# Expert layers: which engine makes the low parts of the weight blocks, and when the router's ranks are issued

## The chip, the cores and the metric

The kernel runs on one core of a Trainium2 chip. The core's engines work side by side, each through its own queue in order: TensorE (matmuls; PE, and PEld for its weight loads), VectorE (DVE), ScalarE (ACT), GpSimd (POOL) and SyncE (SP, which here issues DMAs). They wait for one another through semaphores. The metric is the device time of one execution in microseconds; the time before is a median of three runs.

## What is computed

```python
def reference(**kwargs):
    attn_out = _attn_ref(r, k, v, w, u)          # a recurrence over 768 steps, 4 x 8 heads of 48
    x = attn_out.transpose(0, 2, 1, 3).reshape(3072, 384)
    x = _moe_ref(x, w_gate, w1, w2)              # first expert layer
    return _moe2_ref(x, modality_id, w_gate, modality_bias, w1, w2)   # second one

def _moe_ref(x, w_gate, w1, w2):
    logits = x @ w_gate                          # second layer: + modality_bias[modality_id]
    expert_idx = np.argmax(logits, axis=1)       # one of 8 experts for each token
    gate_w = softmax(logits) at expert_idx
    for e in range(8):
        mask = expert_idx == e
        h = np.maximum(x[mask] @ w1[e], 0.0)     # 384 -> 1024
        out[mask] = gate_w[mask, None] * (h @ w2[e])   # 1024 -> 384
```

## The kernel before

Attention (class `Attn`) runs first, in an order written out by hand (`manual_schedule`), over 24 steps. The two expert layers (class `Moe`) follow; their first pieces are already issued among the last steps of attention. Outside the part ordered by hand, the compiler's list scheduler may move an instruction within its engine's queue ahead of earlier ones that are not ready in its own simulation; what follows is the program's order.

Tokens are sorted by expert into tiles: big ones of 256 tokens ("b") and small ones of 128 ("s"). Layer one has 12 big and 4 small, layer two 12 big and 1 small; three big tiles of each layer are "early", planned from the tokens known by then. Each tile needs its expert's weights: 8 blocks of 128 x 768 float32. `Moe.load` (L375) fetches a block into one of five `raw` buffers on SP's queue. `Moe.split` (L384) then makes two matrices of it that TensorE can multiply fast: the high part `hi`, a rounded copy by ScalarE (L395), and the low part `lo = raw - hi` (L397), by GpSimd for some blocks and by VectorE for the others:

```python
POOL_LO = (1, 3, 5, 7)                                                      # L32
eng = nc.gpsimd if ch in ((1, 4) if short else POOL_LO) else nc.vector      # L396
eng.tensor_tensor(lo[:, s], raw, hi[:, s].bitcast(F32), op=ALU.subtract)    # L397
```

`short` is set in small tiles. The low part is the last reader of its raw buffer. There are two weight buffers, so in `Moe.run` (L484) the blocks of the next tile are split (`sp`) while the present one is multiplied: in a big tile two after each of the blocks 3 and 4 of the first product and two after each half of the second; in a small one 2, 3 and 3.

A big tile is four blocks of the first product (`g1_big`, L425: 18 matmuls; ScalarE makes the high part of h, L440, VectorE the low one, L441), then two halves of the second product (`g2`, L468: 24 matmuls each; ScalarE writes y, L482). Between them `mid` issues gathers of later tiles (`gather`, L399, indirect DMAs on GpSimd's queue) and turns the next tile's tokens (`xprep`, L406). A small tile is `g1_small`, `ht_small` and one `g2`.

Behind the first three blocks and the two halves stands a `tick` (four ticks in a small tile). Each tick runs one piece of the tile before this one (`prev`, from `post1` or `post2`) and two pieces of the planning (`side`). What is left of `prev` is run at the tile's end. In layer one `post1` (L1022) routes the tile's results for layer two with `Router.group` (L125): a piece ends at each `yield`. The pieces of a two-row tile are: transposes (L135); logits (L141); turning them back, maximum, `rt_eq` and the one-hot `oh` (L148 to L167); the ranks `R` on TensorE from `oh` (L170 to L173) and the running sums; and a last piece with slots, `ol` (L196) and the gate (L200), after which the rows are written to `x2s` on SP's queue (L1026). When all tiles of a set have been routed, `early` or `plan` works out which tokens and which expert each tile of layer two has; the loads and gathers of those tiles come after it. All of the router's small products use one PSUM buffer (`pl`).

`moe.open` is False while attention is issued and True from then on.

Of the kernel before, what the change touches and what calls it, by code (L numbers as in the profile page):

```python
# [13 lines left out]
AF = mybir.ActivationFunctionType  # L14
# [17 lines left out]
POOL_LO = (1, 3, 5, 7)  # L32
# [9 lines left out]
def drain(g):  # L42
    for _ in g:
        pass
# [39 lines left out]
def bc(ap, shape):  # L84
    return ap.to_broadcast(shape)


class Router:
# [36 lines left out]
    def group(self, sp, pt, pl, rows, n, k, act, N=4, bias=None, tok=None):  # L125

        nc, c, v = self.nc, self.c, self.nc.vector
# [36 lines left out]
        if tok is not None:  # L164
            val = sp.tile([P, N, 1], F32, name="rt_val", bufs=2)[:, :n]
            v.tensor_scalar(val, tok, float(NTOK), None, op0=ALU.is_lt)
            v.tensor_tensor(oh, oh, bc(val, sh), op=ALU.mult)  # L167
        yield
        R = pl.tile([P, 512], F32, name="pl")[:, :n * E].rearrange("p (a e) -> p a e", a=n)
        nc.tensor.matmul(R, c.tri, oh, start=True, stop=False)  # L170
# [26 lines left out]
        s = sp.tile([P, N, 1], F32, name="rt_s", bufs=2)[:, :n]  # L197
# [168 lines left out]
class Moe:  # L366
# [14 lines left out]
        raw = t.raw[ch] = self.bufs.get("raw")  # L381
        nc.sync.dma_start(raw, t.w[bass.ds(t.er * P, P), ch * CW:(ch + 1) * CW])

    def split(self, t, ch, short=False):  # L384
        nc = self.nc
        if ch == 0:
            w = self.bufs.get("w")
            t.wt = (w[:, 0, :], w[:, 1, :])
        hi, lo = t.wt
        raw = t.raw.pop(ch)  # L390
        s = slice(ch * CW, (ch + 1) * CW)
        if short and ch in ():
            nc.vector.tensor_copy(hi[:, s], raw)
        else:
            nc.scalar.activation(hi[:, s], raw, AF.Copy)  # L395
        eng = nc.gpsimd if ch in ((1, 4) if short else POOL_LO) else nc.vector  # L396
        eng.tensor_tensor(lo[:, s], raw, hi[:, s].bitcast(F32), op=ALU.subtract)  # L397

    def gather(self, t):  # L399
# [84 lines left out]
    def run(self, tiles):  # L484

        seq = [(t, ch) for t in tiles for ch in range(NCH)]
        pos, nl, ng = [0], [0], [0]

        def ahead():
            while nl[0] < min(len(seq), pos[0] + len(self.bufs.ring["raw"])) and seq[nl[0]][0].known("ei"):  # L490
                self.load(*seq[nl[0]])
                nl[0] += 1

        def sp(k=1, short=False):
            for _ in range(k):
                ahead()
                if pos[0] < len(seq):
                    assert pos[0] < nl[0]
                    self.split(*seq[pos[0]], short)
                    pos[0] += 1  # L500
                ahead()

        def gathers(i):
            while ng[0] < len(tiles) and ng[0] <= i and tiles[ng[0]].known() and (ng[0] < NEARLY or self.open):
                self.gather(tiles[ng[0]])
                ng[0] += 1

        def tick():
            for _ in range(self.PT):
                next(prev, None)  # L510
            for _ in range(self.ST):
                next(self.side, None)

        ahead()
        gathers(1)
        yield
        sp(2 if tiles[0].kind == "b" else NCH)
        yield
        gathers(1)
        yield  # L520
        self.xprep(tiles[0])
        yield
        first = True
        prev = iter(())
        for i, t in enumerate(tiles):
            nxt = tiles[i + 1] if i + 1 < len(tiles) else None
            self.hook(t)
            h = self.new_h()

            def mid():  # L530
                if nxt and not nxt.known():
                    drain(self.side)
                gathers(i + 2)
                if nxt:
                    assert ng[0] > i + 1
                    self.xprep(nxt)
            gathers(i + 1)
            if t.kind == "b":
                for fp in range(4):
                    if first and fp > 0:  # L540
                        sp(2)
                    self.g1_big(t, fp, h)
                    if fp < 3:
                        tick()
                    if not first:
                        sp(0 if fp < 2 else 2)
                    yield
                if first:
                    sp(2)
                while not self.open:  # L550
                    yield
                mid()
                yield
                self.g2(t, 0, h)
                tick()
                sp(2)
                yield
                self.g2(t, 1, h)
                tick()
                sp(4 if first else 2)  # L560
                yield
            else:
                ready = nxt and nxt.known()
                if ready:
                    mid()
                h0 = self.g1_small(t, 0)
                tick()
                h1 = self.g1_small(t, 1)
                self.ht_small(0, h0, h)
                self.ht_small(1, h1, h)  # L570
                tick()
                sp(2, True)
                tick()
                self.g2(t, 0, h, 0, 4)
                if not ready:
                    mid()
                sp(3, True)
                self.g2(t, 0, h, 4, 8)
                tick()
                sp(3, True)  # L580
                yield
            for _ in prev:
                next(self.side, None)
            while i + 2 < len(tiles) and not tiles[i + 2].known("hi"):
                next(self.side)
            prev = t.post(t)
            first = False
        for _ in prev:
            pass
# [410 lines left out]
def build(tc, nc, dm, tk, u, uw, wg1, W1, mod, wg2, bias, W2, out):  # L1000
    NBU, NSU1, NSU2 = 12, 4, 1
    v = nc.vector
    with ExitStack() as ctx:
# [42 lines left out]
        with ExitStack() as ac:  # L1046
# [67 lines left out]
            def tail():  # L1114
                early = r1.early(wk, pl)
                yield next(early)
                moe.bufs.add(pool("mright", 1, mst, side="right"), w=1, raw=3, xg=2, x=2, h=1, y=1)
                run = moe.run(seq1 + seq2)
                yield next(run)
                yield next(early)  # L1120
                yield next(run)
                yield from early
                yield from run
# [143 lines left out]
```

## Time and profile before

| | |
|---|---|
| time, median of 3 | 770.69 us (770.32 to 772.57) |
| the profiled execution's own time | 773.58 us |
| its span, first to last instruction | 771.7 us |
| busy in the span: TensorE | 687.5 us, 89% |
| VectorE | 555.3 us, 72% |
| ScalarE | 421.0 us, 55% |
| GpSimd | 405.7 us, 53% |
| mean granted clock of TensorE | 0.95 |
| low parts on GpSimd / on VectorE | 108 / 124 |

Busy time of an engine includes time in which an instruction has started and stands still. Matmuls are pipelined, and their ends are modelled. The share of the granted clock is that of full speed; its two levels are 1.2 and 2.4 GHz. A wait is put down to what came last ahead of it. Layer one lies at about 240 to 550 us of the span, layer two behind it.

### The profile page before, as it was taken

What the parts mean: (1) busy time and instruction counts of PE and PEld (TensorE: products, weight loads), DVE (VectorE), ACT (ScalarE), POOL (GpSimd) and SP (SyncE); (2) the same over time, 40 slices, a digit from 0 to 9 for tenths busy, and PEclk for the clock granted to TensorE, in tenths of its full rate; (3) what the DMA queues carried; (4) which work ended last, traced back from release to release, by engine and by line L of the source; (5) the groups of instructions that cost most, each with busy time, mean ns of one, the idle gap of its engine ahead of it and who ended that gap; (6) DMA issues with size and microseconds to landing.
All of it is one profiled execution on the core that took longest, in us unless ns stands there. A gap on an engine that the chain in (4) does not pass through costs nothing.

```text
span 771.7 us, 15530 instructions
## 1 busy us (share of the span) xinstructions
PE 687.5 (89%) x5528; PEld 625.1 (81%) x5528; DVE 555.3 (72%) x1149; ACT 421.0 (55%) x805; POOL 405.7 (53%) x318
## 2 busy tenths in 40 slices
PE   3788898799699897999899999889998999999992
PEld 1477676687498787999898898868997999999992
DVE  6799888988666787876887878868863766655410
ACT  2357465653444674667576665546364755566520
POOL 4676544453423674553645454345459876676610
PEclk9689899999799998999999999989998999999996
DMA  8695645512645685865775874574377877676400
GB/s 203 179 289 156 180 115 161 175 51 91 200 126 185 215 282 198 267 201 184 247 245 155 260 250 151 199 232 134 106 256 248 278 223 228 224 226 200 151 31 8
DMA packets 55198, 144.91 MB, mean 188 GB/s; under 512 B 6890, under 2 KB 15740, under 8 KB 55112
## 3 DMA queue, kind: packets, MB, share of 16 engines
q1 hardware_dynamic: 50120, 128.26, 53.8%
q0 software_dynamic: 4992, 15.58, 6.3%
q8 instruction: 45, 0.74, 0.4%
q14 instruction: 41, 0.34, 0.1%
HBM read 125.16 MB, written 18.84 MB: 187 GB/s over the span
## 4 chain that ended last, share of the span: by engine, by line
PE 41%; DVE 12%; DMA 6%; issue 4%; ACT 2%; POOL 2%; SPq 1%; POOLq 0%; ACTq 0%
PE py L477 19%; PE pg L436 17%; DMA raw<-in_W_dram 4%; DVE w L397 4%; DVE rt_eq L158 2%; ACT w L395 2%; DVE rt_L L152 2%; DMA out_dram<-y,si 1%; PE pt L416 1%; PE pg L452 1%; POOL w L397 1%; DVE h L441 1%; PE pl L141 1%; POOL xg L404 1%; DMA xg<-x2s,idxe 1%
## 5 line engine op out<-in xcount | busy, mean ns | idle before, releaser
L397 POOL TENSOR_TENSOR w<-raw,w 128x768 fp32r<-128x768 f32 x108 | 207.5, 1928 | 148.2 <-ACT w L395 140.1
L395 ACT ACTIVATE w<-raw 128x768 fp32r<-128x768 f32 x232 | 194.7, 846 | 134.3 <-DMA raw<-in_W_dram 59.7
L477 PE MATMUL py<-w,h 128*128 128x384 f32 x1272 | 242.4, 343 | 5.8 <-ACT h L440 3.0
L397 DVE TENSOR_TENSOR w<-raw,w 128x768 fp32r<-128x768 f32 x124 | 169.6, 1369 | 104.0 <-ACT w L395 103.4
L436 PE MATMUL pg<-x,w 128*128 128x256 f32 x1728 | 231.8, 289 | 2.9 <-DVE h L441 2.2
L477 PEld LDWEIGHTS py<-w,h 128*128 128x128 f32 x1272 | 221.9, 191 | 9.9 <-ACT h L440 3.2
L436 PEld LDWEIGHTS pg<-x,w 128*128 128x128 f32 x1728 | 218.6, 194 | 8.8 <-issue 3.5
L441 DVE SCALAR_TENSOR_TENSOR h<-pg,h 128x512 fp32r<-128x512 f32 x96 | 64.8, 681 | 11.4 <-ACT h L440 11.1
L440 ACT ACTIVATE h<-pg 128x512 fp32r<-128x512 f32 x96 | 56.1, 586 | 14.2 <-PE pg L436 14.2
L1032 POOL DMA_INDIRECT out_dram<-y,si x25 | 31.6, 1264 | 42.1 <-ACT y L482 32.7
L678 POOL TENSOR_TENSOR K<-dm,G 112x512 f32<-112x512 f32 x24 | 28.4, 1185 | 46.9 <-DVE G L671 15.7
L733 PE MATMUL pg<-R,K 64*128 64x128 f32 (+1 forms) x384 | 38.3, 303 | 16.2 <-DVE vd L723 13.9
L733 PEld LDWEIGHTS pg<-R,K 64*128 64x128 f32 (+1 forms) x384 | 30.9, 201 | 26.6 <-DVE vd L723 16.3
L482 ACT ACTIVATE y<-py,xg 128x384 f32<-128x384 f32 x53 | 30.4, 575 | 34.7 <-PE py L477 26.8
L693 POOL TENSOR_TENSOR R<-dm,Fw 112x512 f32<-112x512 f32 x23 | 29.2, 1268 | 36.7 <-DVE Fw L690 34.2
L404 POOL DMA_INDIRECT xg<-xd,idx x22 | 24.3, 1104 | 26.1 <-DVE rt_eq L158 18.5
L128 ACT ACTIVATE lxT<-pt 128x512 f32<-128x512 f32 (+2 forms) x47 | 22.9, 520 | 23.2 <-PE pt L135 23.2
L690 DVE TENSOR_TENSOR_SCAN Fw<-dm,d1r 112x520 f32<-112x520 f32 x24 | 35.0, 1460 | 0.1
L671 DVE TENSOR_TENSOR_SCAN G<-dm,d1k 112x520 f32<-112x520 f32 x24 | 32.9, 1371 | 2.7 <-DMA dm<-in_dm_dram 2.2
L683 POOL TENSOR_TENSOR rk<-dm 112x512 f32<-112x512 f32 x24 | 33.5, 1397 | 0.0
L750 ACT ACTIVATE KT<-pt 128x448 f32<-128x448 f32 x20 | 10.9, 545 | 41.3 <-PE pt L748 41.3
L739 DVE TENSOR_TENSOR M<-pg,mask 128x512 f32<-128x512 f32 x48 | 30.8, 681 | 0.9 <-PE pg L733 0.4
(204 smaller groups left out, 895.8 us busy)
## 6 DMA issues: line engine op xcount, KB each, us to landing
raw<-in_W_dram SPq DMA_DIRECT2D x232, 384.0 KB, 3.8
dm<-in_dm_dram SPq DMA_DIRECT2D x23, 675.5 KB, 4.9
va<-in_tk_dram SPq DMA_DIRECT2D x24, 256.0 KB, 4.2
x2s<-y SPq DMA_DIRECT2D x12, 400.0 KB, 3.1
xd<-x SPq DMA_DIRECT2D x5, 800.0 KB, 4.5
x2s<-z SPq DMA_DIRECT2D x16, 200.0 KB, 5.8
xd<-x SPq DMA_DIRECT2D x2, 400.0 KB, 2.7
x2s<-y SPq DMA_DIRECT2D x4, 200.0 KB, 3.9
```

Of the source, the lines that this page charges most:

```text
L395: nc.scalar.activation(hi[:, s], raw, AF.Copy)
L397: eng.tensor_tensor(lo[:, s], raw, hi[:, s].bitcast(F32), op=ALU.subtract)
L404: self.nc.gpsimd.indirect_dma_start(t.xg[:, a, :], None, t.src, bass.IndirectOffsetOnAxis(ap=idx, axis=0))
L436: nc.tensor.matmul(ps[:, fi, :], w[:, s], x[:, k].rearrange("p a t -> p (a t)"), start=(n == 0), stop=(n == 8))
L440: nc.scalar.activation(hi, ps, AF.Relu)
L441: nc.vector.scalar_tensor_tensor(lo, ps, 0.0, hi.bitcast(F32), op0=ALU.max, op1=ALU.subtract)
L477: nc.tensor.matmul(ps, x[:, f, a, :], w[:, s], start=(f == 0 and i == 0), stop=(f == 7 and i == 2))
L671: v.tensor_tensor_scan(G[:, ::-1], s.w[:, ::-1], self.d1k[:, ::-1], 0.0, op0=ALU.mult, op1=ALU.add)
L683: self.nc.gpsimd.tensor_tensor(s.rk, s.r, s.k, op=ALU.mult)
L690: v.tensor_tensor_scan(Fw, s.w, s.d1, 0.0, op0=ALU.mult, op1=ALU.add)
L733: nc.tensor.matmul(s.ps[h][:, p * P:(p + 1) * P], s.K[rows, p, :], s.R[rows, p, :], start=True, stop=True)
L1032: nc.gpsimd.indirect_dma_start(out, bass.IndirectOffsetOnAxis(ap=si[:, a_:a_ + 1], axis=0), t.y[:, a_, :D], None, bounds_check=NTOK - 1, o ...
```

## The change

Once `open` is True, the low parts of all blocks are made by VectorE; until then the blocks in `POOL_LO` stay on GpSimd, as before. The argument `short` goes, with a branch that was never taken. In `Router.group`, for the second layer's router alone (`tok is not None`), a second `yield` stands between `oh` and the ranks, so that one piece is empty and the ranks and the last piece are issued one tick later.

```diff
@@ Router.group
             v.tensor_scalar(val, tok, float(NTOK), None, op0=ALU.is_lt)
             v.tensor_tensor(oh, oh, bc(val, sh), op=ALU.mult)
+            yield
         yield
         R = pl.tile([P, 512], F32, name="pl")[:, :n * E].rearrange("p (a e) -> p a e", a=n)
         nc.tensor.matmul(R, c.tri, oh, start=True, stop=False)
@@ Moe.split
-    def split(self, t, ch, short=False):
+    def split(self, t, ch):
...
-        if short and ch in ():
-            nc.vector.tensor_copy(hi[:, s], raw)
-        else:
-            nc.scalar.activation(hi[:, s], raw, AF.Copy)
-        eng = nc.gpsimd if ch in ((1, 4) if short else POOL_LO) else nc.vector
+        nc.scalar.activation(hi[:, s], raw, AF.Copy)
+        eng = nc.gpsimd if ch in POOL_LO and not self.open else nc.vector
         eng.tensor_tensor(lo[:, s], raw, hi[:, s].bitcast(F32), op=ALU.subtract)
@@ Moe.run
-        def sp(k=1, short=False):
+        def sp(k=1):
...
-                    self.split(*seq[pos[0]], short)
+                    self.split(*seq[pos[0]])
...
-                sp(2, True)
+                sp(2)
...
-                sp(3, True)
+                sp(3)
...
-                sp(3, True)
+                sp(3)
```

## Rows read from the trace of the kernel before

**Rows 1.** Busy time by stage: stretch, its length, each engine, clock, DMA, GB/s

```profile
240.00:560.00 320.00, 294.65 (x2065) 273.81 (x2064) 254.06 (x582) 190.51 (x331) 161.60 (x109) 0.98 0.66 210
560.00:600.00 40.00, 36.79 (x266) 35.79 (x265) 21.74 (x37) 23.43 (x38) 29.09 (x21) 0.91 0.79 257
600.00:740.00 140.00, 140.00 (x1005) 140.00 (x1004) 83.19 (x88) 82.66 (x126) 95.81 (x59) 1.00 0.66 208
```

**Rows 2.** TensorE's waits, 240 to 560 us: total us, times, longest

```profile
PE pl L170 <- DVE oh L167: 13.4, 9, 4.5
PE pt L416 <- DMA xg<-x2s,idxe: 3.2, 2, 2.1
PE pg L436 <- DVE h L441: 1.9, 2, 1.0
```

**Rows 3.** TensorE's waits, 560 to 760 us

```profile
PE py L477 <- ACT h L440: 3.0, 1, 3.0
```

**Rows 4.** Timeline, 642 to 650 us: start, us, engine, line, operation [idle before]

```profile
642.07 0.96 DVE L397 TENSOR_TENSOR w<-raw,w 128x768 fp32r<-128x768 f32 x1 [2.81 <-ACT w L395]
...
644.23 0.99 POOL L404 DMA_INDIRECT xg<-x2s,idx  x1 [0.31 <-issue]
...
645.23 1.86 POOL L397 TENSOR_TENSOR w<-raw,w 128x768 fp32r<-128x768 f32 x1
645.30 2.62 DVE L397 TENSOR_TENSOR w<-raw,w 128x768 fp32r<-128x768 f32 x1 [2.27 <-ACT w L395]
...
649.17 2.37 PE L436 MATMUL pg<-x,w 128*128 128x256 f32 x18
```

**Rows 5.** Groups by line: times, busy us, mean ns, idle before and its releasers

```profile
L397 POOL TENSOR_TENSOR w<-raw,w 128x768 fp32r<-128x768 f32 x108 | 207.5, 1928 | 148.2 <-ACT w L395 140.1 <-PE pl L173 4.3 <-DMA raw<-in_W_dram 3.1
...
L397 DVE TENSOR_TENSOR w<-raw,w 128x768 fp32r<-128x768 f32 x124 | 169.6, 1369 | 104.0 <-ACT w L395 103.4
...
L158 DVE SCALAR_TENSOR_TENSOR rt_eq<-rt_L,eneg 128x16 f32<-128x16 f32 x14 | 15.4, 1100 | 0.3
...
L152 DVE TENSOR_TENSOR rt_L<-rt_L,xg 128x16 f32<-128x16 f32 x12 | 9.1, 755 | 0.2
```

**Rows 6.** Timeline, 419 to 425 us: one late `oh`

```profile
419.62 3.94 DVE L158 SCALAR_TENSOR_TENSOR rt_eq<-rt_L,eneg 128x16 f32<-128x16 f32 x1
419.88 3.63 POOL L397 TENSOR_TENSOR w<-raw,w 128x768 fp32r<-128x768 f32 x2
...
424.24 0.18 PE L170 MATMUL pl<-oh,tri 128*128 128x16 bf16 x1 [1.65 <-DVE oh L167]
```

**Rows 7.** Busy time of line 397 alone by stage: VectorE, GpSimd, clock, DMA, GB/s

```profile
240.00:560.00 320.00, 98.89 (x77) 120.11 (x62) 0.98 0.66 210
600.00:740.00 140.00, 52.94 (x32) 61.04 (x32) 1.00 0.66 208
```

**Rows 8.** Timeline, 581 to 595 us: a run of low parts and a stall

```profile
581.42 5.46 POOL L397 TENSOR_TENSOR w<-raw,w 128x768 fp32r<-128x768 f32 x3
...
587.03 0.85 ACT L395 ACTIVATE w<-raw 128x768 fp32r<-128x768 f32 x1 [5.58 <-DMA raw<-in_W_dram]
...
594.28 4.21 PE L436 MATMUL pg<-x,w 128*128 128x256 f32 x18 [0.26 <-DVE h L441]
```

**Rows 9.** Timeline, 418 to 420 us: a gather beside a low part

```profile
418.06 0.94 DVE L397 TENSOR_TENSOR w<-raw,w 128x768 fp32r<-128x768 f32 x1
418.24 1.63 POOL L404 DMA_INDIRECT xg<-xd,idx  x1 [0.81 <-DVE rt_m L155]
```

**Rows 10.** Busy time and clock, 295 to 305 us, columns as rows 1

```profile
295.00:305.00 10.00, 8.62 (x38) 7.96 (x38) 6.96 (x21) 1.99 (x3) 0.88 (x3) 0.66 0.68 233
```

**Rows 11.** Waits of VectorE, GpSimd and ScalarE, 240 to 560 us

```profile
DVE w L397 <- ACT w L395: 39.0, 35, 2.7
POOL w L397 <- ACT w L395: 91.3, 34, 8.3
ACT y L482 <- DMA x2s<-y: 7.7, 4, 2.2
```

## The prediction

> **What bounds the kernel now.** I read the stage table first, because the average over the whole span mixes an attention half, in which the changed lines hardly run, with two expert layers that have different limits. From 600 to 740 us TensorE is busy for 140.00 of 140 us at full granted clock: the second layer, once its plan exists, is bound by TensorE, and nothing that VectorE or GpSimd do faster is worth anything there. From 240 to 560 us TensorE is busy for 294.65 of 320, and from 560 to 600 for 36.79 of 40, at 0.98 and 0.91 of the granted clock [rows 1]. So 25.4 + 3.2 = 28.6 us of idle TensorE, and a few more of slowed clock, are all that this change can win.
>
> Then I asked what ended that idle time. In 240 to 560 us the largest entry by far is the first matmul of the router's ranks (L170) waiting for the one-hot tile `oh` of VectorE (L167): 13.4 us in nine waits. The gathers of the second layer's first tile follow with 3.2 us, the low part of h with 1.9 [rows 2]. After 560 us one wait of 3.0 us for ScalarE's h stands out [rows 3].
>
> Last I asked why VectorE is late, although it is not full. A low part on VectorE alone takes 0.96 us. The one at 645.30, beside a GpSimd low part that began 0.07 us earlier and took 1.86, took 2.62: VectorE stood still until GpSimd was through, and then did its work [rows 4]. The group rows carry the same: 1369 ns in the mean for 124 low parts on VectorE against 0.96 us alone, and `rt_eq`, an operation on 16 elements, has a mean of 1100 ns [rows 5]. One of these explains a wait of TensorE from end to end: `rt_eq` began at 419.62, two GpSimd low parts ran from 419.88 to 423.51, `rt_eq` ended at 423.56, and the rank matmul, which needed `oh` three small operations later, began at 424.24 after 1.65 us of idle [rows 6]. So GpSimd's low parts cost VectorE much of the time that they keep from its queue.
>
> **Part 1: the low parts move to VectorE.** Of 108 on GpSimd those of the blocks split while `open` is still False stay: the first tile's four, and one of the second's if its first two blocks are still issued then. About 103 move; each takes 1928 ns on GpSimd [rows 5] and 0.96 on VectorE [rows 4].
>
> What that does to VectorE's load in the first layer: 98.89 us for 77 low parts, with 62 more on GpSimd [rows 7]. Afterwards 139 x 0.96 = 133.4, so 34.6 more. Against it stand the stalls of other operations: `rt_eq` goes from 1100 to about 170 ns, 14 x 0.93 = 13.0 less; the bias addition `rt_L` from 755 to about 160 ns, 12 x 0.6 = 7.2 less [rows 5]. So 254.06 + 34.6 - 20.2 = 268.5 us at most, and less by whatever the remaining small operations lose to GpSimd now, which I estimate at up to as much again, 20: 248 to 268, as against 254 now. VectorE is no fuller than before; the same time is spent on work rather than on standing still. In the steady second layer it goes from 83.19 to 83.19 - 52.94 + 64 x 0.96 = 91.7 of 140 us [rows 1, 7], under a TensorE that is full: nothing. If that cover failed, and each of the eight tiles there had one low part of h behind one more low part, it would cost 8 x 0.96 = 8 us; the range has room for it.
>
> The raw buffers come free sooner, since the low part is their last reader and takes half as long. That matters where three GpSimd low parts in a row (5.46 us from 581.42) held buffers: ScalarE then stood 5.58 us for the next raw block, its h was queued behind that block, and TensorE idled 3.0 us. After it, 18 matmuls took 4.21 us which elsewhere take 2.37 [rows 3, 4, 8]; the granted clock of this stretch is 0.91 [rows 1]. This stall costs 3.0 + 1.8 = 4.8 us, and goes: the three low parts would take 2.9 us on VectorE, which is busy for 21.74 of the 40 us [rows 1]. Should the raw blocks' own transfers be late next, 0 to 4.8 of it would stay; I take 0, because the wait followed GpSimd's run of three at once.
>
> GpSimd keeps its copies and indirect transfers. A gather overlapped by a VectorE low part took 1.63 us against 0.99 alone [rows 4, 9], so up to 0.64 more for each. It is issued a tile ahead; this shows only at the hand-over between layers, where two gathers in a row are waited for: 0 to 1.3 us.
>
> The Trainium skill speaks to that last price. SBUF — State Buffer, section "Who interferes with whom", says that a two-input VectorE operation takes only the read side of the pair that it shares with GpSimd, so that writing descriptors should not be held up (marked there as inferred). By it this term would be 0 at both ends; the row of 1.63 us disagrees, and the row decides.
>
> **Part 2: the ranks one piece later.** An empty piece is put between `oh` and the ranks in the second layer's router. All of the rank piece moves by a tick: two or three small matmuls on TensorE's queue, the sums on VectorE; and the last piece with about a dozen small VectorE operations and, on SP's queue, the write to `x2s`. A tick in a big tile is one block of 18 matmuls, 2.37 us [rows 4]. The waits on `oh` are 1.5 us in the mean (13.4 / 9) [rows 2], so one tick covers most of them; the one of 4.5 needs part 1 as well. In a small tile, with four ticks, ranks and last piece both go to the end of the tile; in a big one only the last piece does, with the second layer's planning a tick later in program order. I take 11 of the 13.4 us as won, keeping 2.4 for waits at tile ends. The 4.5 us wait also cost clock: from 295 to 305 us the grant was 0.66, 3.4 us of work lost [rows 10], of which about 0.7 lay in idle time, so 2.7 more.
>
> What it may cost. The later `x2s` write holds the buffers of y: ScalarE now waits 7.7 us in four waits for that write [rows 11]; a tick more on each would be 9.5 us of ScalarE, which has 130 of 320 us free [rows 1], so 0 on the end if other work is ahead. At the hand-over the first gathers of the second layer wait for such a write, and TensorE for them 3.2 us [rows 2]; here a tick can cost its full 2.37, and below nothing a shorter VectorE queue can bring the write forward by as much. With the gathers' 0 to 1.3 that is -2.4 to +3.7; I take +3.0, near the upper end, since nothing else is queued to cover it.
>
> **The sum.** -11 (waits for `oh`) - 2.7 (clock after them) - 4.8 (stall at 590) - 1 (half of the low parts of h, 1.9) + 3 (hand-over) = -16.5 us. The profiled execution took 773.58 us with a span of 771.7, 2.9 above the median of 770.69; applied there it gives a span of 755.2, and the same difference from the median gives 754.2 us.
>
> **Rivals.**
> *VectorE's queue becomes the bound of layer one.* An engine does its work in order. GpSimd waited 91.3 us in 34 waits for ScalarE's high parts and hurt nobody; VectorE waited 39.0 in 35 [rows 11]. If the moved blocks bring such waits along in proportion, 39.0 x 139 / 77 = 70.4, the router and h stand behind them. VectorE is not busy for 320 - 254 = 66 us of the stage now [rows 1]; with all of the growth it would last 248 to 268 + 66 + 31, so 345 to 365 us. That is an upper bound, since a fuller VectorE comes later to the same wait; half the growth, 16 us, on the middle of the load gives 258 + 66 + 16 = 340, 20 more than now: 771 + 20 - 5 (the stall at 590) = 786 us. It decides as soon as VectorE's idle time in this stage stays above 320 - 258 = 62 us instead of shrinking. Against it: ScalarE's h stands in that same order already, and 42 of VectorE's 77 low parts found their high part done.
> For it speaks the Trainium skill, Perfetto Trace Analysis, section "Optimizing Scalar/DVE Operations": when VectorE is saturated, handing work to GpSimd may pay, though the two share a port. The stage table bears out the sharing more than the saturation.
> *Only the second stall goes; the waits for `oh` turn into others of the same length* (h behind two low parts, 1.9 us; a later hand-over). Then -4.8 + 3 and little else: 769 us, no change to be told.
> *Half of it*: layer one wins 6 instead of 14.7: 762 us.
> *All of it*: 28.6 + 2.7 + 1.8 = 33 us, 738 us; against it, the 3.2 us at the hand-over wait for transfers, which no engine shortens [rows 2].
> *It doesn't do what it says*: if TensorE's waits for `oh` had been caused by its own order and not by GpSimd, part 2 alone would still take most of them; this falls together with the half.
>
> **How the numbers follow.** Forecast 754 (746 to 760): 0.58. Half: 0.16. All, or nearly: 0.07. No change: 0.08. VectorE as the bound: 0.11 (a sum of 1). The range from 741 to 769 leaves out the slower case, the part of the unchanged case above 769 and the far end of the full gain, under 0.2. The measurement tells about 0.3%, 2.3 us, from no change: faster 0.81, same 0.08, slower 0.11.
>
> **What would show it.** Right: no low part of VectorE above about 1.6 us after 240 us and `rt_eq` near 0.17 us throughout; waits of L170 for `oh` under 3 us in all; no TensorE gap near the tile that first uses the second layer's plan; VectorE's busy time in the first layer about as long as now. Wrong: TensorE's waits for the low part of h or for VectorE's `rt_` operations rising above 10 us; a longer gap ahead of the second layer's first transposes; VectorE's waits for ScalarE growing past 60 us in layer one; or a first layer that is not shorter although VectorE's stalls are gone, which would make raw transfers the bound.

## The result and the profile after

| | before | after |
|---|---|---|
| median | 770.77 us (765.32 to 774.30, 14 runs) | 763.02 us (760.33 to 767.51, 14 runs) |
| ratio, 95% | | 0.9917 (0.989 to 0.9944) |
| the profiled execution's own time | 773.58 us | 761.14 us |
| its span | 771.7 us | 759.4 us |
| GpSimd busy | 405.7 us | 198.1 us |
| VectorE busy | 555.3 us | 542.6 us |

By the medians the change makes the kernel 7.8 us faster (by the ratio 6.4, between 4.3 and 8.5), where 16.7 had been forecast. The time lies in the wider range of 741 to 769, near the "half" rival, and outside the forecast's own 746 to 760. The two profiled executions are 12.4 us apart: that of before was 2.8 above its median, that of after 1.9 below. So a ledger from one pair of profiles carries some 4.7 us that the medians don't bear out, and I use it for where the time went, and the medians for how much. Below, executions in a slower state of the chip (one of `p2_rank_only`, some of the kernel before) are left out of medians and ratios.

What the change does to the engines came as expected. Groups by line of after (busy us, mean ns, then idle time ahead and its releasers), against [rows 5]:

```profile
L395 DVE TENSOR_TENSOR w<-raw,w 128x768 fp32r<-128x768 f32 x227 | 215.9, 957 | 79.8 <-ACT w L393 72.0 <-PE py L475 6.5 <-issue 0.2
...
L395 POOL TENSOR_TENSOR w<-raw,w 128x768 fp32r<-128x768 f32 x5 | 9.1, 1827 | 19.6 <-ACT w L393 15.3 <-DMA xd<-x 4.3
...
L158 DVE SCALAR_TENSOR_TENSOR rt_eq<-rt_L,eneg 128x16 f32<-128x16 f32 x14 | 2.4, 173 | 0.3
```

The low part on VectorE went from 1369 to 957 ns and `rt_eq` from 1100 to 173: in the expert layers VectorE hardly stands still beside GpSimd any more. So VectorE does 103 more low parts and is busy for less. Stage table of after, columns as [rows 1]:

```profile
240.00:560.00 320.00, 300.97 (x2141) 282.11 (x2140) 239.37 (x652) 197.41 (x339) 40.93 (x48) 0.96 0.68 217
560.00:600.00 40.00, 37.48 (x279) 36.56 (x278) 30.09 (x42) 27.81 (x42) 15.48 (x14) 1.00 0.90 309
600.00:740.00 140.00, 138.87 (x971) 137.17 (x969) 76.59 (x107) 74.84 (x117) 25.55 (x25) 1.00 0.57 180
```

VectorE fell from 254.06 to 239.37 us in the first layer, and TensorE is busier there, but the granted clock went down, from 0.98 to 0.96. Fixed stretches of time mix what was done with when, so I cut both traces at the same instructions: the plan of layer one (L299 before, L300 after), the first product of layer one's last small tile (L452, L450), the plan of layer two, and the end. Before first, then after, columns as [rows 1]; behind a stretch's two times stand its length and TensorE's busy time, with the number of matmuls:

```profile
239.00:504.56 265.56, 246.62 (x1746) 230.09 (x1745) 211.51 (x466) 163.80 (x283) 136.60 (x91) 0.99 0.70 220
504.56:554.83 50.27, 43.86 (x295) 39.55 (x294) 38.25 (x94) 26.32 (x47) 25.43 (x18) 0.93 0.56 175
554.83:771.70 216.87, 199.32 (x1395) 196.57 (x1393) 112.06 (x153) 111.47 (x173) 127.83 (x82) 0.96 0.58 185
```

```profile
237.83:485.56 247.73, 242.78 (x1746) 229.46 (x1745) 193.22 (x505) 165.29 (x281) 31.82 (x37) 0.99 0.73 233
485.56:548.67 63.11, 49.02 (x325) 43.59 (x324) 38.21 (x119) 28.74 (x52) 8.43 (x10) 0.86 0.47 151
548.67:759.40 210.73, 192.99 (x1364) 189.58 (x1363) 117.95 (x189) 109.49 (x170) 43.99 (x42) 0.97 0.59 190
```

The first stretch holds 1746 matmuls in both and is 17.8 us shorter: TensorE's idle time (length less busy) falls from 18.9 to 5.0, and the same matmuls take 3.8 us less. The second, the hand-over between the layers, is 12.8 us longer: idle time rises from 6.4 to 14.1; 30 matmuls more lie in it, which at 0.142 us each (242.78 / 1746) are 4.3 us of work done earlier. The third is 6.1 us shorter, but 4.4 of that are the 31 matmuls that are gone from it; its idle time stays (17.6 and 17.7, of which 13.8 and 13.6 lie behind the last matmul), and the clock gives the rest. In all, TensorE idles 36.8 us from the plan of layer one on, where it idled 42.9: of the 14.0 won in layer one, 7.9 are lost again behind it.

TensorE's waits in the hand-over of after, 485.56 to 548.67 us (total, times, longest), against [rows 2]:

```profile
PE pl L171 <- DVE oh L167: 9.8, 3, 4.8
PE pt L414 <- DMA xg<-x2s,idxe: 2.9, 2, 2.4
PE pl L148 <- ACT lg L128: 0.6, 1, 0.6
```

In layer one no wait for `oh` is left (12.0 us in seven before); all three are now here. The timeline of this stretch in after (start, us, engine, line, operation [idle before]):

```profile
485.87 0.16 DVE L229 SCALAR_TENSOR_TENSOR idxe<-pl,pl_pm 128x6 int32<-128x6 f32 x1
...
487.64 0.25 PE L148 MATMUL pl<-ident,lg 96*128 96x96 f32 x1
...
493.25 0.58 ACT L453 ACTIVATE hs<-pg 128x512 f32<-128x512 f32 x1
...
494.60 0.15 DVE L167 TENSOR_TENSOR oh<-oh,rt_val 128x8 bf16<-128x8 bf16 x1
...
494.81 0.19 PE L171 MATMUL pl<-oh,tri 128*128 128x8 bf16 x1 [4.83 <-DVE oh L167]
...
495.08 10.59 SPq L1024 DMA_DIRECT2D x2s<-y  x2
...
500.17 0.58 ACT L480 ACTIVATE y<-py,xg 128x384 f32<-128x384 f32 x1 [3.24 <-DMA x2s<-y]
500.64 0.21 ACT L160 ACTIVATE rt_ex<-rt_L 128x16 f32<-128x16 f32 x1
500.86 0.97 POOL L402 DMA_INDIRECT xg<-x2s,idxe  x1 [32.96 <-ACT rt_ex L160]
500.88 0.17 DVE L199 TENSOR_REDUCE rt_s<-rt_ex 128x2 f32<-128x16 f32 x1 [2.05 <-ACT rt_ex L160]
...
501.40 0.20 PE L171 MATMUL pl<-oh,tri 128*128 128x16 bf16 x1 [3.84 <-DVE oh L167]
...
504.01 0.69 PE L414 MATMUL pt<-ident,xg 128*128 128x128 f32 x2 [2.36 <-DMA xg<-x2s,idxe]
...
511.54 0.60 PE L461 MATMUL pt<-ident,hs 128*128 128x128 f32 x4
```

And the same steps before:

```profile
499.51 0.25 PE L148 MATMUL pl<-ident,lg 96*128 96x96 f32 x1
...
503.77 0.17 DVE L167 TENSOR_TENSOR oh<-oh,rt_val 128x8 bf16<-128x8 bf16 x1
...
506.88 0.98 POOL L404 DMA_INDIRECT xg<-x2s,idxe  x1 [3.76 <-DVE rt_rr L182]
...
511.88 0.58 ACT L455 ACTIVATE hs<-pg 128x512 f32<-128x512 f32 x1
...
521.56 0.60 PE L463 MATMUL pt<-ident,hs 128*128 128x128 f32 x4
```

Read down both. The last small tile's product came 19.0 us earlier; the router's logits, which need the `pl` buffer that the early plan holds until `idxe`, 11.9 (499.51 to 487.64); `oh`, with four low parts now between its small operations on VectorE, 9.2; the first gather from `x2s`, which follows the write of those rows, 6.0. Last, the small tile's own transposes: its `hs` was ready at 493.83, but they ran only at 511.54, because `mid` had put the transposes of layer two's first tile (L414) ahead of them, and those wait for that gather; the router's own (L135, at 507.64 and 510.84) went ahead of them too, all through the same two `pt` buffers. Before, the same hold was there (512.46 to 521.56), but 9.1 us long instead of 17.7. The plan of layer two needs this tile's routing, and comes 47.8 us after the gather (47.95 before): 6.2 us earlier, not 19. The second wait for `oh` (3.84 us) has another origin than the first: ScalarE stood 3.24 us for the write to `x2s` before it could reuse a buffer of y, `rt_ex` came behind that y in its queue, and VectorE's next operation, which `oh` follows, waited for `rt_ex`. ScalarE's waits for that write in the hand-over, after and then before:

```profile
ACT y L480 <- DMA x2s<-y: 5.1, 2, 3.2
```

```profile
ACT y L482 <- DMA x2s<-y: 1.4, 1, 1.4
```

During the hold TensorE had little to do, and the clock fell: from 490 to 505 us it is busy for 2.81 of 15 us, at a grant of 0.58, so near the lower of its two levels (1.2 GHz).

```profile
490.00:505.00 15.00, 2.81 (x15) 1.07 (x15) 9.16 (x42) 4.58 (x10) 2.12 (x3) 0.58 0.64 209
505.00:520.00 15.00, 14.28 (x93) 12.71 (x94) 5.24 (x11) 6.71 (x12) 2.12 (x3) 0.85 0.18 56
```

### The profile page after: what moved, and what is told of

Its sections match the earlier page's. It is cut to its first block, busy times and chain, and to the rows that moved or that the text cites. A ratio compares the mean times of both kernels' runs of the same rounds, so it can differ in the third digit from the quotient of the medians.

```text
span 759.4 us, 15541 instructions
## 1 busy us (share of the span) xinstructions
PE 681.8 (90%) x5528; PEld 621.2 (82%) x5528; DVE 542.6 (71%) x1252; ACT 422.9 (56%) x805; POOL 198.1 (26%) x215
## 5 line engine op out<-in xcount | busy, mean ns | idle before, releaser
L395 DVE TENSOR_TENSOR w<-raw,w 128x768 fp32r<-128x768 f32 x227 | 215.9, 957 | 79.8 <-ACT w L393 72.0
L475 PE MATMUL py<-w,h 128*128 128x384 f32 x1272 | 237.6, 339 | 1.8 <-DVE h L439 1.1
L475 PEld LDWEIGHTS py<-w,h 128*128 128x128 f32 x1272 | 218.9, 188 | 5.2 <-DVE h L439 2.2
L439 DVE SCALAR_TENSOR_TENSOR h<-pg,h 128x512 fp32r<-128x512 f32 x96 | 65.5, 683 | 7.6 <-ACT h L438 7.4
L438 ACT ACTIVATE h<-pg 128x512 fp32r<-128x512 f32 x96 | 56.1, 586 | 19.5 <-PE pg L434 18.6
L1030 POOL DMA_INDIRECT out_dram<-y,si x25 | 25.9, 1037 | 149.4 <-ACT y L480 131.2
L731 PE MATMUL pg<-R,K 64*128 64x128 f32 (+1 forms) x384 | 38.4, 304 | 16.8 <-DVE vd L721 13.8
L691 POOL TENSOR_TENSOR R<-dm,Fw 112x512 f32<-112x512 f32 x23 | 29.2, 1268 | 36.6 <-DVE Fw L688 34.2
L1028 DVE CAST si<-xg 128x2 int32<-128x2 f32 (+1 forms) x13 | 2.2, 172 | 40.7 <-DMA out_dram<-y,si 30.2
```

The costliest lines, as they stand in the source:

```text
L438: nc.scalar.activation(hi, ps, AF.Relu)
L439: nc.vector.scalar_tensor_tensor(lo, ps, 0.0, hi.bitcast(F32), op0=ALU.max, op1=ALU.subtract)
L475: nc.tensor.matmul(ps, x[:, f, a, :], w[:, s], start=(f == 0 and i == 0), stop=(f == 7 and i == 2))
L731: nc.tensor.matmul(s.ps[h][:, p * P:(p + 1) * P], s.K[rows, p, :], s.R[rows, p, :], start=True, stop=True)
```

## The experiments

Each was timed beside the kernel before, whose median in those rounds was within 0.4 us of 770.77; a ratio is to the kernel before in the same rounds, and small differences between medians of different rows say little. For each, the idle time of TensorE in the three stretches above (length less busy, in us), worked out from its own rows as for before and after. They are of one execution each, which lay up to 4.5 us from its kernel's median:

| kernel | layer one | hand-over | behind the plan | sum | plan at | median us | ratio, 95% |
|---|---|---|---|---|---|---|---|
| before | 18.9 | 6.4 | 17.6 | 42.9 | 554.8 | 770.77 | 1 |
| after | 5.0 | 14.1 | 17.7 | 36.8 | 548.7 | 763.02 | 0.9917 (0.989 to 0.9944) |
| p1_low_only | 7.1 | 12.7 | 16.7 | 36.5 | 550.3 | 762.39 | 0.9874 (0.9843 to 0.9905) |
| p2_rank_only | 18.4 | 5.2 | 18.1 | 41.8 | 548.3 | 767.80 | 0.9978 (0.9949 to 1.0007) |
| hand_pool | 11.9 | 8.2 | 16.5 | 36.6 | 550.2 | 762.52 | 0.9875 (0.9843 to 0.9906) |
| early_pt | 16.8 | 0.3 | 23.8 | 40.9 | 549.9 | 768.36 | 0.998 (0.9943 to 1.0017) |
| last5 | 15.7 | 1.6 | 25.7 | 43.0 | 551.2 | 771.80 | 0.9989 (0.9956 to 1.0022) |
| last5_ne4 | 14.4 | 5.0 | 19.9 | 39.4 | 556.5 | 767.33 | 0.9939 (0.9905 to 0.9972) |
| before_last5 | 12.8 | 7.5 | 19.5 | 39.8 | 549.7 | 767.18 | 0.9953 (0.9914 to 0.9991) |
| late_mid | 6.7 | 10.8 | 15.2 | 32.7 | 534.5 | 758.19 | 0.9801 (0.9758 to 0.9843) |
| src32 | 7.6 | 8.7 | 24.9 | 41.2 | 549.6 | 766.30 | 0.995 (0.992 to 0.998) |
| src32_late | 7.2 | 9.7 | 15.9 | 32.8 | 536.7 | 757.17 | 0.9846 (0.9806 to 0.9885) |
| before_src32_late | 18.7 | 5.5 | 20.3 | 44.5 | 558.8 | 771.92 | 1.0018 (0.9982 to 1.0054) |
| p1_src32_late | 6.6 | 9.8 | 17.3 | 33.7 | 536.3 | 759.20 | 0.9861 (0.9822 to 0.99) |

The sum orders the medians almost without exception: from 44.5 us (771.9) to 32.7 (758.2), 1.2 us of time for each us idle. Its parts don't: idle time goes from one stretch into another.

**Which part pays.** `p1_low_only` is after without the extra `yield` in `Router.group`; `p2_rank_only` is before with nothing but that `yield`.

> Part 1 alone: all low parts on VectorE once open is True, no extra piece in the router. Theory A (the hand-over hole comes with the moved low parts, because TensorE's queue then holds two routers back to back and VectorE's low parts stand between their small operations): TensorE idle at the hand-over stays 10 us or more, L170 waits 8 us or more there, layer one before it as tight as with both parts; time 761 to 766. Theory B (the hole comes from the ranks being a piece later): the hole shrinks to the 5 us or so of the kernel before, but some waits for oh come back in layer one; time 752 to 758.

> Part 2 alone: the ranks a piece later, low parts shared with GpSimd as in the kernel before. Theory A: most of the 13.4 us of waits for oh in layer one goes (half or more), the hand-over stays as before, the stall near 590 us stays; time 762 to 768. Theory B: waits in layer one go likewise, but a hole of 10 us or more opens at the hand-over; time 770 to 776. If instead VectorE's stalls beside GpSimd were the cause and a tick is no cover, the waits stay and the time is 769 to 772.

Part 1 alone gives all of it: 762.39 against 763.02 us with both. Part 2 alone gives 1.7 us by the ratio (from 3.9 faster to 0.5 slower), not clear of zero. TensorE's waits in `p2_rank_only`, 240 to 560 us, and then behind:

```profile
PE pl L171 <- DVE oh L167: 8.2, 6, 1.7
...
PE py L478 <- DVE h L442: 2.5, 1, 2.5
```

```profile
PE py L478 <- ACT h L441: 3.1, 1, 3.1
```

The waits for `oh` fall from 13.4 to 8.2 us, others take their place (layer one idles 18.4 us instead of 18.9), and the stall at 590 us stays. One tick does not cover the waits; taking GpSimd's low parts away does. The longer hand-over is in `p1_low_only` too (12.7 us idle, two waits for `oh` of 8.5 us), so it comes with part 1, not with the later ranks.

**Is the wait for `oh` at the hand-over the cause?** `hand_pool` gives the low parts of the two last tiles of layer one and the two first of layer two back to GpSimd, so that they don't stand between the router's small operations:

```diff
-        eng = nc.gpsimd if ch in POOL_LO and not self.open else nc.vector
+        eng = nc.gpsimd if ch in POOL_LO and (not self.open or t in self.hand) else nc.vector
...
+        moe.hand = seq1[-2:] + seq2[:2]
```

> The changed kernel, with the low parts of blocks 1, 3, 5 and 7 of the four tiles around the hand-over (the last two of layer one, the first two of layer two) back on GpSimd. Theory A1 (VectorE's queue of low parts between the router's small operations makes oh late there): the waits for oh at the hand-over fall from 9.8 to under 4 us, time 752 to 758. Theory C (the routers wait because the early plan holds the only pl buffer, whoever makes the low parts): the hole stays within 3 us of the changed kernel's, time 761 to 766.

In the hand-over the waits for `oh` went (one of 3.3 us is left ahead of it), but the time stayed: 762.52 us, with 36.6 us idle in all, as in after. Neither theory had both: A1 asked for 752 to 758 us, C for a hole that stays. Its three stretches, and two waits of its hand-over, show where it idles instead:

```profile
239.70:497.22 257.52, 245.66 (x1746) 232.13 (x1745) 196.89 (x509) 165.56 (x283) 52.16 (x48) 0.97 0.71 228
497.22:550.24 53.02, 44.79 (x304) 40.91 (x304) 36.15 (x91) 27.60 (x49) 19.53 (x16) 0.90 0.52 161
550.24:764.60 214.36, 197.82 (x1384) 194.56 (x1383) 121.19 (x198) 109.35 (x170) 43.71 (x42) 0.97 0.58 187
```

```profile
PE pt L135 <- DVE rt_L L152: 3.0, 1, 3.0
PE pl L300 <- DVE rt_rr L183: 2.5, 1, 2.5
```

The hand-over is 53 us long where it was 63, but layer one, whose last two tiles also got their low parts back on GpSimd, is 9.8 us longer; the last small tile starts 11.7 us later than in after, and the plan comes no sooner (550.24 against 548.67). Other matmuls that wait for VectorE stand at the head of TensorE's queue in place of the one for `oh`. So taking that wait away brought nothing here; what it is worth by itself the run doesn't show, since the edit moved the end of layer one as well.

**Is it the early plan, which holds `pl`, or the early gather?** Three ways to have layer two's first rows sooner: `early_pt` gives the early plan's products to the `pt` buffers (`r2.early(sp, pt, "pt")`), `last5` starts that plan one tile sooner, `src32` tells the early gathers that they read only the first 32 x 128 rows of `x2s`, so that they don't wait for later writes:

```diff
-LAST = 4
+LAST = 5
```

```diff
-            return Tile(r2, kind, j, W2, x2s, post2, early)
+            return Tile(r2, kind, j, W2, x2s[:1 + 32 * P] if early else x2s, post2, early)
```

> The changed kernel, with the early plan's two products in the pt buffers instead of the single pl buffer, so that the routers need not wait for it. Theory C: the router of the last small tile but one no longer starts only after the plan's last product; the three routers spread over the hand-over, the waits for oh there fall from 9.8 to under 3 us, the first gather of layer two comes 5 us or more earlier against the small tile before it, time 750 to 756. Theory A1: the routers run earlier but still late one by one, 758 to 763.

> The changed kernel with LAST 5 instead of 4: the early plan of layer two starts one tile earlier, behind a big tile's router instead of the second small one's. Theory C (the serial chain early plan in the single pl buffer, then the held router, its x2s write, the first gather, is too late now that layer one is shorter): the plan's buffer is free before the last three tiles' routers come, the first gather of layer two starts 8 us or more sooner against the last small tile's first product, the waits for oh and the gather at the hand-over fall from 12.7 to under 5 us; time 750 to 757. Theory A1 (VectorE's low parts between the router's operations make oh late wherever it stands): waits of 8 us or more stay, time 760 to 765.

> The changed kernel, where the early gathers of layer two read only the first 32 blocks of rows of x2s, all that they need; the last small tile but one writes behind them, so the first gather no longer waits for that tile's write. Theory E (the hole is a chain: early plan, router of that small tile, its x2s write, first gather, and all that stands behind the gather): the first gather starts at about 487 instead of 500.9 us of the span, the transposes of layer two's first tile run in the hole, TensorE's idle time from 480 to 520 us falls from 12.9 to under 7; time 750 to 757. Theory A1 (low parts between the router's operations, whatever the gather does): the wait of 4.8 us for oh and most of the hole stay, 760 to 764.

All three moved the gather (to 481.17, 492.37 and 489.27 us, from 500.86; in `src32` TensorE could use it only at 500.53, where it was 504.01) and none made the kernel faster than after: 768.36, 771.80 and 766.30 us, outside the ranges of both theories each time (for `src32` the intervals of the ratios still overlap with that of after). The hand-over's idle time falls to 0.3, 1.6 and 8.7 us, and one hole opens behind the plan. TensorE's first wait there, in `src32`:

```profile
PE pt L414 <- DMA xg<-x2s,idx: 9.9, 2, 9.2
```

In `last5` the same wait is 10.5 us in two, in `early_pt` 8.8 in one. The plan comes no sooner (549.6 to 551.2 us), so the three tiles that the early plan feeds are used up before the plan's own gathers land. `last5_ne4` makes them four (`NE2` = 4 beside `LAST` = 5), and `before_last5` is the same step on the kernel before:

> LAST 5 and four early tiles in layer two instead of three, so that TensorE has one big tile more (17.5 us) while the second plan is made. If the earlier hand-over only moves the hole to the second plan (raw blocks and gathers that wait for it), this one is faster than last5 by 4 us or more, 748 to 754; if not, both agree within 2 us.

> A control: the kernel before with LAST 5. By theory C its first hand-over was not late but for some 5 us (3.2 us wait for the first gather, clock), so it gains 2 to 5 us: 766 to 769. If LAST 5 were good by itself, whatever the low parts, it would gain as much as the changed kernel does from it (8 us or more).

The fourth tile takes the hole down (25.7 to 19.9 us idle behind the plan; 767.33 us, 4.5 less than `last5`), but the time is not below that of after, nor in the range forecast. On the kernel before, `LAST` = 5 is worth 3.6 us (767.18), as expected: there TensorE reaches the end of layer one later, which I take for the reason.

**Is it the order of the transposes?** `late_mid` lets the last small tile of layer one prepare the first tile of layer two only behind half of its second product, so that its own transposes and its routing don't stand behind a gather:

```diff
-                ready = nxt and nxt.known()
+                ready = nxt and nxt.known() and nxt.r is t.r
```

> The changed kernel, with the last small tile of layer one preparing layer two's first tile (transposes in the pt buffers) behind half of its second product instead of ahead of its first product. Theory D (the small tile's own transposes, L461, are held behind the first gather because they come later in the ring of pt buffers): its transposes run before the gather lands, some 4 to 6 us of TensorE's work fill the hole, time 756 to 760. Theory C alone: the hole stays within 2 us, time 761 to 766.

758.19 us, as the theory of the hold had it. Its interval (0.9758 to 0.9843) lies wholly below that of after. Timeline:

```profile
492.26 0.57 ACT L453 ACTIVATE hs<-pg 128x512 f32<-128x512 f32 x1
...
499.09 0.58 ACT L480 ACTIVATE y<-py,xg 128x384 f32<-128x384 f32 x1 [3.08 <-DMA x2s<-y]
...
499.72 1.54 PE L135 MATMUL pt<-ident,y 128*128 128x128 f32 x6 [3.07 <-ACT y L480]
499.78 0.97 POOL L402 DMA_INDIRECT xg<-x2s,idxe  x1 [32.37 <-ACT rt_ex L160]
...
501.58 1.12 PE L461 MATMUL pt<-ident,hs 128*128 128x128 f32 x4 [0.26 <-ACT lxT L128]
...
509.33 0.60 PE L414 MATMUL pt<-ident,xg 128*128 128x128 f32 x4
```

The gather is issued about when it was (499.78 against 500.86), but the small tile's transposes run at 501.58 instead of 511.54, ahead of L414, and the plan comes at 534.51 instead of 548.67, 34.7 us after the gather instead of 47.8. The hold is shorter, not gone: 8.7 us instead of 17.7, now behind the router's transposes (L135), which wait for ScalarE's y and so for the write to `x2s`. TensorE's idle time falls by 4.1 us in all, the median by 4.8 (the ratios lie further apart, 0.9917 and 0.9801). The profiled execution was 4.5 us below this kernel's median, so its span of 751.9 us is not the figure to go by.

Last, the two edits together, on after (`src32_late`), on before (`before_src32_late`) and on part 1 alone (`p1_src32_late`):

> Both hand-over edits on the changed kernel: the shorter source of the gathers, and layer two's first tile prepared behind half of the last small tile's second product. If both act on the same hole (theory E with D), the time is that of the better one within 2 us, 751 to 758; if they are separate, 748 to 752.

> Control: the same two edits on the kernel before. By theory E and D its hand-over has only some 5 us to give, since layer one is as long as the chain there: 765 to 769. If the edits were good whatever the low parts, they would gain as much here as on the changed kernel (5 us or more against 770.8, so below 766).

> Both hand-over edits with part 1 alone (no extra piece in the router). If part 2 is worth something once the hand-over is no longer the limit, this one is 2 us or more slower than src32_late; if VectorE without GpSimd's low parts makes oh in time anyway, both agree within 2 us.

On after 757.17 us, not to be told from `late_mid`; with `late_mid` it is the fastest version here. On the kernel before the same two edits give nothing, not even the few us expected (771.92, interval around 1): there the hold was 9.1 us long, and TensorE idled 6.4 us in the whole hand-over. So the longer hold came with the shorter layer one. That the hold cost nothing before is not quite shown, since this control has the edit of `src32` in it too, which on after didn't help. Without part 2 the time is 759.20, within the intervals: part 2 adds nothing that can be measured here either.

## Why the prediction was right and wrong

**The bound and the mechanism: right.** TensorE idled in layer one for the router's `oh`, VectorE was late because it stood still beside GpSimd's low parts, and moving them cures it: `rt_eq` at 173 ns, no wait for `oh` left in layer one, VectorE less busy than before. It fell further than I put it (239 us against 248 to 268). The Trainium skill, Perfetto Trace Analysis, section "Optimizing Scalar/DVE Operations", on which the main rival leaned, offers GpSimd where VectorE is saturated, and warns that between these two it might not help because of their shared port. Here the warning held: taking 103 operations back from GpSimd left VectorE 15 us less busy in the stage.

**Layer one (-14.7): a little too small by this pair.** On equal work the ledger has -14.0 of idle time and -3.8 of slower matmuls, 17.8 us. Leaving out the kernels that move the early plan or give low parts back to GpSimd, those with part 1 idle 5.0 to 7.6 us in layer one and those without 18.4 to 18.9; so 11 to 14 us of idle time are won, and after lies at the good end. The split between the parts was wrong: I gave the tick of part 2 most of the 11 us, and alone it takes away 0.5 us of layer one's idle time.

**The stall at 590 us (-4.8): only the clock came.** The wait of 3.0 us for ScalarE's h is gone, and the granted clock from 560 to 600 went from 0.91 to 1.00. But the idle time behind the plan is 17.7 us as against 17.6. The waits there now, 548.67 us to the end:

```profile
PE py L475 <- DVE h L439: 1.1, 2, 0.7
PE pt L414 <- DMA xg<-x2s,idx: 1.1, 1, 1.1
PE pg L434 <- ACT x L415: 1.1, 1, 1.1
```

The first is small waits of another kind, the other two the plan's first gather and what hangs on it. Of 4.8 us, 1.9 came: 1364 matmuls at 0.1415 us instead of 0.1429.

**The hand-over (+3): this is the step that failed.** I priced it by one tick of delay (2.37) and slower gathers (0 to 1.3), as if its length stayed and only its start moved. It cost 7.7 us of idle time and, with the lower clock, some 8.5 (63.1 - 50.3, less 4.3 for the 30 matmuls done earlier). The delay was not the extra tick, since `p1_low_only` has it too; nor the gathers, whose mean was 997 ns where it was 1173. What went was cover, time in which TensorE had other work: the chain early plan, routing, write, gather, then the last small tile's own routing, then the plan is made of latencies, and TensorE had been late enough to hide most of it. I asked "what is late next" of the stall at 590 and not of the 14.7 us themselves. I had written "a longer gap ahead of the second layer's first transposes" among the signs of being wrong, and that is the one that came. `late_mid` shows it: with the hold cut by 9.0 us, the plan comes 13.1 us sooner after the gather, and the median of after falls by 4.8 us. A second term of the same step was put at nothing, the later write to `x2s` that holds the buffers of y ("0 on the end if other work is ahead"): at the hand-over ScalarE's wait for it went from 1.4 to 5.1 us, and a wait of TensorE for `oh` of 3.84 us hangs on it. What that costs by itself no run shows.

**The sum.** By the profiled pair: 1.2 us that lie ahead of layer one's plan, 17.8, less 8.5, and 1.8 make 12.3 us of span (16.5 forecast): the hand-over took 5.5 us more than its term and the stall gave 3.0 less, against 3.1 more from layer one and the 1.2 ahead of it. The other 4.5 us, from 12.3 to the 7.8 of the medians, stand in no row: the two profiled executions lie on opposite sides of their medians, 4.7 us in all, and which stretches vary is not shown. The forecast did not allow for this in its own range of 746 to 760.

**The rivals.** *VectorE's queue as the bound* fell. VectorE's waits for ScalarE's high parts in 240 to 560 us, against [rows 11]:

```profile
DVE w L395 <- ACT w L393: 43.8, 53, 2.2
```

From 39.0 they went to 43.8 us, not to 70. The sign that I gave for it was badly chosen: VectorE is idle for 80.6 us of the stage, above my 62, but because it has less to do. *Only the second stall goes* fell with layer one. *Half of it* has the right time, 762 us, for another reason: by the profiled pair layer one won more than the forecast, and what followed gave it back. *All of it* failed at the hand-over. *It doesn't do what it says* fell with `p2_rank_only`.

**What stays open.** In `late_mid` TensorE still idles 10.8 us in the hand-over, with 5.2 us of waits for `oh` and 3.1 for ScalarE's y at the head of its queue; I have not tried to remove this, and `hand_pool` doesn't tell what such a wait is worth. Nor did I run `late_mid`'s edit alone on the kernel before, or find why `last5` and `early_pt` idle 11 to 12 us more in layer one than after.

## What to carry to other kernels

When a stage gets shorter, look for the chain of latencies that starts in it and ends in the next: price the hand-over by that chain's length less the work that covers it, not by the delay that the edit adds. The operation at the head of an in-order queue is not the cause until taking its wait away moves the time; cut both traces at the same instructions and compare the sums of idle time, since idle time moves from stretch to stretch. And see which buffer ring or queue puts independent work behind a transfer: putting it ahead cost one condition here and was worth more than half as much as the change itself (4.8 and 7.8 us of the medians).

## What the runs showed of the hardware

A two-input operation of VectorE beside a two-input one of GpSimd stands still until that is through [rows 4, 6], however small it is: `rt_eq` on 16 elements had a mean of 1100 ns with GpSimd's low parts and 173 without. The operation that makes the low part of h (L441 before, L439 after), which reads one of its inputs from PSUM, kept its time, 681 and 683 ns. The other way round, a gather's issue is stretched, as the forecast had it from [rows 9]; in `late_mid`

```profile
509.20 2.00 DVE L395 TENSOR_TENSOR w<-raw,w 128x768 fp32r<-128x768 f32 x2 [1.28 <-ACT w L393]
509.30 1.70 POOL L402 DMA_INDIRECT xg<-x2s,idxe  x1 [7.07 <-ACT w L393]
```

it took 1.70 us beside two low parts, against 0.97 at 499.78 with none. The Trainium skill (SBUF — State Buffer, "Who interferes with whom") infers that writing descriptors is not held up by a two-input VectorE operation. That inference is not refuted: a gather also reads its row numbers (`idxe`) from SBUF, and no run here tells the reading from the writing. What after shows is that it matters which came first. Of GpSimd's indirect issues in the expert layers that had a low part beside them, none that began ahead of it was stretched (0.94 to 1.02 us), and all that took more than 1.05 us (up to 1.71) had begun while one was under way, as in the rows above and in [rows 9]. What I had not expected is that over the kernel this doesn't add up: GpSimd's indirect writes of the output went from 1264 to 1037 ns in the mean.
